# A planned instruction order for a convolution and two small networks on one core: durations of the plan, lent buffers, and the lag of the last network

## The chip, the core and the metric

The kernel runs on one core of one Trainium2 chip. The metric is the device time of one execution in microseconds (us). A core has five engines that run side by side and each take their instructions strictly in the order in which the program gives them: PE (TensorE, matrix products; its weight loads are listed apart as PEld), DVE (VectorE), ACT (ScalarE), POOL (GpSimd) and SP (SyncE, which here only issues transfers). Engines wait for each other through semaphores. PE writes into PSUM, eight banks of 128 x 512 32-bit values; all else lies in SBUF.

## The reference

For two sequences of 4160 tokens with 192 channels, three layers follow each other (shapes are batch, token, channel):

```python
# 1: a weighted sum over a window of 7 tokens, weights by softmax, 8 heads of 24 channels
w = exp(wg - max(wg)) ; w = w / (sum(w) + 1e-9)
x = einsum("bshk,bskhg->bshg", w, windows(x))
# 2: a mix of each token with the one before it, a network of width 1024, a gate
xk = mu_k * x + (1 - mu_k) * x_prev ; xr = mu_r * x + (1 - mu_r) * x_prev
x = sigmoid(xr @ w_r) * (maximum(xk @ w_k, 0) ** 2 @ w_v)
# 3: a network of width 1024 with a convolution of three tokens as its gate
h = maximum(x @ w_in, 0)
g = sigmoid(sum(conv_w[k] * shifted(h, k) for k in range(3)))
out = (h * g) @ w_out
```

Everything is 32-bit floating point.

## The kernel before

The tokens of each sequence are cut into ten tiles of 256, 220, seven times 476, and 352 tokens. A product is made precise by splitting its operands into a high and a low part (the cast to `fp32r` is the high part, the subtraction after it the low part), so that each product of the two networks takes five matmuls instead of two. For one tile and one batch the work is this:

- **attention**: POOL multiplies the window rows by the softmax weights and folds the seven products (`prod`, `prod`, `prod`, `tok`), four slots for a tile of 476 tokens.
- **mixing** (three for a tile: `u` is 0, 2 or 1; the second in time is `u = 2`): PE transposes the tokens into a bank `pa` ("flip"), ACT copies the shifted part (`att`), DVE subtracts, DVE writes two mixes (`mk`), ACT casts the high part (`xA`, or `rm` when `u = 2`), POOL subtracts for the low part. When `u = 2`, SP then moves both parts into `xB`.
- **gate_r** and **moe1**, eight steps: five matmuls into a bank `pa` (`xA`, `xB` with `wk`), two ACT passes, an ACT cast and a DVE subtraction (`s`), and five matmuls with `wv` into the banks `am`, `ar`. `gate_r` makes five matmuls with `wr` and a sigmoid (`r`) for each of two channel blocks. `mix_out` multiplies both and leaves `x`.
- **moe2**, eight steps: five matmuls into a bank `pc` (`x` with `wi`), relu and a scaled copy on ACT, two DVE taps of the convolution, a sigmoid, a product, a cast and a subtraction (`g`), and five matmuls with `wo` into `bm`, `br`. `store` copies both banks (`att`, `om`) and SP sends them out.

In the first 90 us or so the weights come in as well: sixteen chunks pass through `stage`, a buffer of 4096 32-bit columns, on ACT, DVE and PE.

No loop sets the order. Every piece of work is filed with a step number (`at(t, fn)`; a moe1 step is one unit of `t`, a tile 16 units). The class `Program` records all instructions, then `schedule` plays them through with a table of durations (`cost`, line 80): at each moment each engine takes, among its instructions that are ready by the table, the one with the lowest step number. The instructions are given to the chip in the order of the start times that come out. The table is thus no duration on the chip, but it decides in which order each engine's queue stands. Two numbers of the plan matter here: moe2 of a tile is filed `LAG` = 11 steps behind its moe1 (lines 31, 841, 844), and the tiles of each ring are handed out in turn, so a write into a tile has to wait for the last reader of what stood there. `mk` has two tiles, `att` two, `om` one (lines 256 to 264). When the weights are through, columns of `stage` from 864 on lie idle, but for two tiles lent to moe2 (`q_r`, line 287).

All instructions are recorded by one helper, so every row of the profile has the line L178; rows are told apart by the names of their tiles.

Of the kernel before, what the change touches and what calls it, by code (L numbers as in the profile page):

```python
# [9 lines left out]
F32R = mybir.dt.float32r  # L10
U32 = mybir.dt.uint32
# [8 lines left out]
NMAX = max(SIZES)  # L20
# [7 lines left out]
PAD = KS - 1  # L28
WIN = KS * DM
NF = DFF // 128  # L30
LAG = 11

S_LAG, G_LAG = 3.25, 4.75
DONE = 16 * NTILE + S_LAG - 0.95
ALONE = 7


def f(ap):
    return ap.bitcast(F32)


class Program:
# [26 lines left out]
    def region(self, ap):  # L69
# [7 lines left out]
            return ap.tensor.name, 0, 128, 0, 512  # L77
        return ap.tensor.name, p0, p0 + dims[0][1], f0, f0 + sum(s * (c - 1) for s, c in dims[1:]) + 1

    def cost(self, eng, method, out, ins, pointer):  # L80

        n = self.count(out)
        src = [self.space(x) for x in ins]
        if method == "dma_start":
            return 0.6, 0.0
        if eng == "PE":
            if method == "matmul" and ins[0].dtype == F32:
                n *= 4.6
            busy = max(n * 0.00045 + 0.002, 0.109)
            return busy, busy + 0.24  # L90
        if eng == "ACT":
            near = bool(src) and src[0] == "PSUM"
            p = 0.1 if pointer else 0.0
            return (0.06 if near else 0.09) + p + n / 1200, (0.2 if near else 0.24) + p + n / 1200
        if eng == "DVE":
            if method == "tensor_reduce":
                return 0.05 + self.count(ins[0]) / 515, 0.15 + self.count(ins[0]) / 515
            if method == "reciprocal":
                return 0.07 + n / 160, 0.2 + n / 160
            if method in ("tensor_scalar", "tensor_copy", "memset") and "PSUM" not in src:  # L100
                return 0.07 + n / 1920, 0.2 + n / 1920
            stt = method == "scalar_tensor_tensor"
            return (0.13 if stt else 0.07) + n / 960, (0.26 if stt else 0.2) + n / 960
        if eng == "POOL":
            busy = 0.15 + (n / 455 if method == "tensor_tensor" else n / 270)
            return busy, busy + 0.1
        return 0.6, 0.6

# [84 lines left out]
def conv_moe_kernel(ctx: ExitStack, tc: tile.TileContext, xp, wg_first, wg_rest, mus, w_k, w_v, w_r, w_in, conv_w, w_out, out):  # L193
# [11 lines left out]
    def ring(name, n, shape, dtype=F32):  # L205
        return Ring([new(f"{name}{j}", shape, dtype) for j in range(n)])

    def bank(name):
        t = ps.tile([128, 512], F32, name=name)
        prog.spaces[t.tensor.name] = "PSUM"  # L210
        return t

    W = NMAX + 4
# [42 lines left out]
    att_r = ring("att", 2, [128, NMAX])  # L256
    mk_r = ring("mk", 2, [128, NMAX])
# [6 lines left out]
    om_r = ring("om", 1, [128, W])  # L264
# [7 lines left out]
    for j in range(4):  # L272
        n = soft_at[j + 1] - soft_at[j]
# [7 lines left out]
    am_r, ar_r, bm_r, br_r = (Ring([bank(x)]) for x in ("am", "ar", "bm", "br"))  # L281
# [3 lines left out]

    spare = f(stage)[:, 2 * (soft_at[4] - soft_at[3]) * NH:]
    q_r = Ring([spare[:, j * W:(1 + j) * W] for j in (0, 1)])
    pt_r = Grow(pc_r.tiles, (16 * NTILE, pa_r.tiles))
    ht_r = Grow(h_r.tiles, (16 * NTILE, mk_r.tiles))
    gt_r = Grow(g_r.tiles, (DONE, s_r.tiles))  # L290
# [3 lines left out]
    def at(t, fn, hold=0.0):  # L294
        plan.append((t, len(plan), fn, hold))
# [205 lines left out]
    def mixing(i, u, t, dt_):  # L501
        N, P, e = SIZES[i], PART[i], EXTRA[i]
        c = 1 if u >= 2 else 0
        O = slice(64 if u == 4 else 0, 64 if u == 3 else 128)
        st = {}

        def flip():
            p = pa_r()
            st["p"] = p[O, e:e + N]
            st["q"] = p  # L510
            x = tok_t[i]
            k, n = ((0, 128), (256, 128), (128, 128), (128, 64), (128, 128))[u]

            for l in reversed(range(SLOTS[i])):
                PE.transpose(p[0:n, l:l + SLOTS[i] * (P - 1) + 1:SLOTS[i]], x[:, l, k:k + n], ident)

        def shifted(fn):
            a = att_r()[O, :N]
            if e:
                fn(a, st["q"][O, e - 1:e + N - 1])  # L520
            else:
                fn(a[:, 1:N], st["q"][O, 0:N - 1])
            return a

        def m0():
            a = st["d"] = shifted(ACT.copy)
            DVE.tensor_tensor(a, a, st["p"], op=ALU.subtract)

        def m1(k):
            st[k] = ar_r.tiles[0][:, 256 * k:256 * k + 256] if i == 0 else mk_r()  # L530
            col = 2 * k + c
            own = slice(col, col + 1)
            if i < 2:
                a = shifted(lambda y, x: ACT.activation(y, x, ACTF.Copy, scale=onemu[O, own]))
                DVE.scalar_tensor_tensor(out=st[k][O, :N], in0=st["p"], scalar=mu[O, own], in1=a, op0=ALU.mult, op1=ALU.add)
            else:
                DVE.scalar_tensor_tensor(out=st[k][O, :N], in0=st["d"], scalar=onemu[O, own],
                                         in1=st["p"], op0=ALU.mult, op1=ALU.add)

        def hi(k):  # L540
            if u < 2:
                x = xA_r[k]()
                xin[i, u, k, 0] = x
            else:
                x = rm_r[k]().unsqueeze(1)
            st["h", k] = x
            ACT.copy(x[O, 0, :N], st[k][O, :N])

        def lo(k):
            x = st["h", k]  # L550
            y = x[O, 1, :N] if u < 2 else (mk_r() if i == 0 else st[k])[O, :N].bitcast(F32R)
            (POOL if i else DVE).tensor_tensor(y, st[k][O, :N], f(x[O, 0, :N]), op=ALU.subtract)
            if u >= 2:
                for b in range(NB) if u == 2 else (u - 3,):
                    z = xB_r[k]()
                    xin[i, b, k, 1] = z
                    own = slice(64 * b, 64 * b + 64)
                    oth = slice(64 - 64 * b, 128 - 64 * b)
                    SP.dma_start(out=f(z[own, :N]), in_=f(x[own, 0, :N]))
                    SP.dma_start(out=f(z[oth, :N]), in_=f(y[own] if u == 2 else y))  # L560

        at(t, flip)
        if i >= 2:
            at(t + 0.1 * dt_, m0)
        at(t + 0.2 * dt_, lambda: m1(0))
        at(t + 0.3 * dt_, lambda: m1(1))
        at(t + 0.4 * dt_, lambda: hi(0))
        at(t + 0.5 * dt_, lambda: lo(0))
        at(t + 0.6 * dt_, lambda: hi(1))
        at(t + 0.7 * dt_, lambda: lo(1))  # L570


# [122 lines left out]
    def moe2(i, b, fi, t):  # L695
# [28 lines left out]
        def c6():  # L724
            st["q"] = q_r() if i >= ALONE else st["p"]
            DVE.tensor_tensor(st["q"][:, :N], st["h"][:, 1:N + 1], st["p"][:, :N], op=ALU.mult)
# [6 lines left out]
        def c8():  # L733
            g = st["g"]
            (POOL if i >= ALONE else DVE).tensor_tensor(g[:, 1, :N], st["q"][:, :N], f(g[:, 0, :N]), op=ALU.subtract)

# [17 lines left out]
    def store(i, b, t):  # L754
        N = UNIT[i]
        last = i == NTILE - 1
        a = 1 if i == 1 else 0
        n = N + (1 if last else 0)
        t0 = STARTS[i] - OFFSET[i] - 1
        st = {}  # L760

        def e0():
            st["b"] = att_r()[0:64]
            ACT.copy(st["b"][:, :n], acc2["r"][64:128, :n])

        def e1():
            st["m"] = om_r()
            ACT.copy(st["m"][:, :n], acc2["m"][:, :n])
            SP.dma_start(out=out[b, 0:128, t0 + a:t0 + n], in_=st["m"][:, a:n])

        def e2():
            DVE.tensor_tensor(st["b"][:, :n], acc2["r"][0:64, :n], st["b"][:, :n], op=ALU.add)
            SP.dma_start(out=out[b, 128:192, t0 + a:t0 + n], in_=st["b"][:, a:n])

        at(t, e0)
        at(t + 0.1, e1)
        at(t + 0.2, e2)
# [36 lines left out]
    for j in range(NTILE - 3):  # L814
        a, b = (sum(slots[3:3 + k]) for k in (j, j + 1))
# [3 lines left out]
    a = slots[3]  # L819
# [6 lines left out]
    for i in range(NTILE):  # L826
# [6 lines left out]
        for b in range(NB):  # L833
# [4 lines left out]
            for fi in range(NF):  # L838
                moe1(i, b, fi, t + fi)
                if i:  # L840
                    moe2(i, b, fi, t + fi + LAG)
            mix_out(i, b, t + S_LAG + 7.27)
            if i:
                store(i, b, t + LAG + G_LAG + 7.27)

# [70 lines left out]
```

## Time and profile before

| | |
|---|---|
| median of three timed runs | 749.13 us (748.6 to 750.31) |
| the profiled execution | 749.3 us, of which the span from first to last instruction is 747.5 us |
| busy share of the span | PE 95%, PEld 81%, ACT 87%, DVE 78%, POOL 73% |
| mean granted clock of TensorE | 0.992 of its full 2.4 GHz |
| matmuls in the trace | 3473 |

Busy shares are means over stages with different limits. PE's matmuls overlap in the trace, so a busy PE is not always a PE at its full pace; how many matmuls start in a stretch tells the pace. The trace has the table of busy times by stretch, who waited for whom, and the instructions in order of time.

### The profile page before, as it was taken

To read this page: it belongs to the slowest core of one execution; us is meant where nothing else is said; L and a number is where in the kernel's file an instruction comes from. 1 tells how busy PE (TensorE), PEld (TensorE's weight loads), DVE (VectorE), ACT (ScalarE), POOL (GpSimd) and SP (SyncE) were. 2 spreads that over 40 slices of the span, in tenths; PEclk is the share of its full clock that TensorE was granted. 3 is DMA by queue.
4 is the path that set the end of the run, shared out by engine and by line. 5 is a ranking of instruction groups with operands and counts; after the bars stand their busy time and mean duration, and the time that the engine had idled before them with its cause. 6 is when DMAs were issued, how large, how long until landed. Compare 5 with 4: busy or idle time off the path is not lost.

```text
span 747.5 us, 10554 instructions
## 1 busy us (share of the span) xinstructions
PE 711.2 (95%) x3473; PEld 606.9 (81%) x3473; DVE 581.2 (78%) x985; ACT 650.0 (87%) x1388; POOL 546.7 (73%) x398
## 2 busy tenths in 40 slices
PE   3898888999999999989999999999999999999996
PEld 2677777888788888878888888888888888889995
DVE  5656968879998978787878787879786767676775
ACT  2588779999989899988989998999899989989986
POOL 3799999997899999999999999996113333333334
PEclk9999999999999999999999999999999999999999
DMA  7678212011211140213120410130003000200000
GB/s 227 171 248 241 75 54 52 6 68 54 72 54 24 49 126 1 72 53 74 53 73 1 126 48 20 48 73 1 20 1 73 0 21 1 59 1 20 1 20 30
DMA packets 18791, 45.09 MB, mean 60 GB/s; under 512 B 2992, under 2 KB 14256, under 8 KB 18608
## 3 DMA queue, kind: packets, MB, share of 16 engines
q1 hardware_dynamic: 18736, 44.41, 20.3%
q8 instruction: 27, 0.44, 0.3%
q14 instruction: 28, 0.23, 0.1%
HBM read 27.40 MB, written 6.39 MB: 45 GB/s over the span
## 4 chain that ended last, share of the span: by engine, by line
PE 48%; POOL 35%; ACT 6%; DVE 4%; issue 4%; DMA 2%; SPq 0%; ACTq 0%; POOLq 0%; DVEq 0%
POOL prod L178 28%; PE pa L178 15%; PE pc L178 10%; PE bm L178 7%; PE am L178 6%; PE br L178 5%; PE ar L178 4%; POOL tok L178 3%; POOL xA L178 2%; DVE pc L178 1%; ACT pa L178 1%; POOL mk L178 1%; DMA stage<-in_moe_w_in_dram 1%; DMA stage<-in_moe_w_k_dram 1%; DVE mk L178 1%
## 5 line engine op out<-in xcount | busy, mean ns | idle before, releaser
L178 DVE SCALAR_TENSOR_TENSOR pc<-h,cw,pc 128x476 f32<-128x476 f32 (+1 forms) x276 | 194.6, 705 | 42.1 <-ACT pc L178 39.1
L178 POOL TENSOR_TENSOR prod<-rows,sw 128x1344 f32<-128x1344 f32 x70 | 216.4, 3093 | 12.6 <-DVE sw L178 10.5
L178 ACT ACTIVATE pa<-pa 128x476 f32<-128x476 f32 (+4 forms) x326 | 163.3, 504 | 29.6 <-PE pa L178 26.0
L178 POOL TENSOR_TENSOR prod<-prod 128x576 f32<-128x576 f32 (+1 forms) x132 | 161.8, 1225 | 9.0
L178 PE MATMUL am<-s,wv 128*128 128x476 f32 (+3 forms) x480 | 142.0, 356 | 2.9 <-ACT s L178 2.8
L178 PE MATMUL bm<-g,wo 128*128 128x476 f32 (+1 forms) x414 | 135.2, 379 | 2.1 <-ACT g L178 1.8
L178 PE MATMUL pa<-xA,wkA 128*128 128x476 f32 (+3 forms) x480 | 123.1, 361 | 3.7 <-DVE s L178 2.6
L178 POOL TENSOR_TENSOR g<-stage,g 128x476 fp32r<-128x476 f32 (+1 forms) x42 | 48.5, 1156 | 96.3 <-ACT g L178 76.0
L178 PE MATMUL pc<-x,wiA 128*128 128x478 f32 (+1 forms) x414 | 113.4, 379 | 0.9 <-ACT x L178 0.4
L178 DVE TENSOR_TENSOR s<-pa,s 128x476 fp32r<-128x476 f32 (+3 forms) x160 | 93.8, 586 | 21.6 <-ACT s L178 20.2
L178 PE MATMUL ar<-s,wv 128*128 128x476 f32 (+3 forms) x320 | 109.1, 355 | 0.0
L178 PE MATMUL br<-g,wo 128*128 128x476 f32 (+1 forms) x276 | 103.4, 376 | 0.0
L178 PEld LDWEIGHTS pa<-xA,wkA 128*128 128x128 f32 x480 | 83.8, 189 | 21.2 <-DVE s L178 7.1
L178 PEld LDWEIGHTS am<-s,wv 128*128 128x128 f32 x480 | 87.0, 188 | 15.0 <-ACT s L178 4.4
L178 ACT ACTIVATE pc<-h,cw 128x476 f32<-128x476 f32 (+1 forms) x138 | 92.0, 667 | 0.7
L178 ACT ACTIVATE h<-pc 128x478 f32<-128x478 f32 (+1 forms) x138 | 78.8, 571 | 12.5 <-PE pc L178 10.6
L178 PE MATMUL pa<-xB,wkB 128*128 128x476 f32 (+3 forms) x320 | 88.7, 357 | 0.0
L178 PEld LDWEIGHTS bm<-g,wo 128*128 128x128 f32 x414 | 76.8, 189 | 13.8 <-ACT g L178 2.7
L178 PEld LDWEIGHTS pc<-x,wiA 128*128 128x128 f32 x414 | 75.5, 189 | 15.3 <-DVE g L178 3.4
L178 ACT CAST s<-pa 128x476 fp32r<-128x476 f32 (+3 forms) x160 | 83.1, 520 | 1.5
L178 DVE TENSOR_TENSOR pc<-h,pc 128x476 f32<-128x476 f32 x96 | 62.8, 654 | 26.9 <-ACT pc L178 26.0
L178 PE MATMUL pc<-x,wiB 128*128 128x478 f32 (+1 forms) x276 | 81.7, 377 | 0.0
(135 smaller groups left out, 1170.0 us busy)
## 6 DMA issues: line engine op xcount, KB each, us to landing
rows<-in_x_dram SPq DMA_DIRECT2D x14, 960.0 KB, 4.6
xB<-rm SPq DMA_DIRECT2D x28, 119.0 KB, 2.3
xB<-mk SPq DMA_DIRECT2D x28, 119.0 KB, 2.3
out_dram<-om SPq DMA_DIRECT2D x14, 238.0 KB, 2.0
rows<-in_x_dram SPq DMA_DIRECT2D x4, 768.0 KB, 5.8
rows<-in_x_dram SPq DMA_DIRECT2D x2, 864.0 KB, 4.7
out_dram<-att SPq DMA_DIRECT2D x14, 119.0 KB, 2.2
stage<-in_moe_w_v_dram SPq DMA_DIRECT2D x4, 384.0 KB, 4.5
```

Of the source, the lines that this page charges most:

```text
L178: getattr(self.real[eng], method)(*a, **k)
```

## The change

It has three parts. The table of durations in `cost` gets other numbers: products of 32-bit operands on PE cost less (a factor of 3.75 for 4.6), single-source passes of DVE lose a double rate, POOL passes in place cost 0.08 us more, and ACT and DVE passes whose output lies on other partitions than their input get a surcharge. From step 20 on three rings are longer: `mk` gets two more tiles, `att` one, `om` one, all in the idle columns of `stage`. `LAG` goes from 11 to 12, so that moe2 and `store` of every tile are filed one step later.

```diff
-LAG = 11
+LAG = 12
+SPARE = 20
...
             if method == "matmul" and ins[0].dtype == F32:
-                n *= 4.6
+                n *= 3.75
...
-            if method in ("tensor_scalar", "tensor_copy", "memset") and "PSUM" not in src:
+            if method == "memset":
                 return 0.07 + n / 1920, 0.2 + n / 1920
...
+    mkt_r = Grow(mk_r.tiles, (SPARE, [spare[:, j * W:j * W + NMAX] for j in (2, 3)]))
+    attt_r = Grow(att_r.tiles, (SPARE, [spare[:, 4 * W:4 * W + NMAX]]))
+    omt_r = Grow(om_r.tiles, (SPARE, [spare[:, 5 * W:6 * W]]))
...
         def shifted(fn):
-            a = att_r()[O, :N]
+            a = attt_r()[O, :N]
...
-            st[k] = ar_r.tiles[0][:, 256 * k:256 * k + 256] if i == 0 else mk_r()
+            st[k] = ar_r.tiles[0][:, 256 * k:256 * k + 256] if i == 0 else mkt_r()
...
         def e0():
-            st["b"] = att_r()[0:64]
+            st["b"] = attt_r()[0:64]
...
-            st["m"] = om_r()
+            st["m"] = omt_r()
```

No instruction is added or taken away; PE has 3431 of them in both programs, DVE 987, ACT 1390, POOL 403, SP 173. What moves is their order, and the tiles that the mixes write.

First place: DVE in the second mixing of the sixth tile (`u = 2`, tile number 5). `mk`, `att`, `stage` are tiles of the rings, `s`, `g`, `pc` belong to moe1 and moe2. Before:

```order
L178 TENSOR_TENSOR att1_88<-att1_88,pa1_114 128x476
L178 TENSOR_TENSOR pc0_115<-h0_109,pc0_115 128x476
L178 SCALAR_TENSOR_TENSOR mk0_89<-att1_88,onemu_62,pa1_114 128x476
L178 TENSOR_TENSOR s0_105<-pa0_113,s0_105 128x476
L178 TENSOR_TENSOR g0_77<-pc0_115,g0_77 128x476
L178 SCALAR_TENSOR_TENSOR mk1_90<-att1_88,onemu_62,pa1_114 128x476
```

With the change, at the same place:

```order
L183 TENSOR_TENSOR stage_76<-stage_76,pa1_114 128x476
L183 SCALAR_TENSOR_TENSOR stage_76<-stage_76,onemu_62,pa1_114 128x476
L183 TENSOR_TENSOR pc1_116<-h1_110,pc1_116 128x476
L183 TENSOR_TENSOR s0_105<-pa0_113,s0_105 128x476
L183 SCALAR_TENSOR_TENSOR stage_76<-stage_76,onemu_62,pa1_114 128x476
L183 TENSOR_TENSOR g3_80<-pc1_116,g3_80 128x476
```

The mixes stand about where they stood, but they write into columns of `stage` instead of into `mk0` and `mk1`, which the first mixing of the same tile has just filled.

Second place: ACT at the end of the second tile and in the second mixing of the third (`u = 2`, tile number 2), around the one exponential of 448 columns that stands between sigmoids (`sw` is the softmax, `r00` the first gate of moe1, `rm` the high part that goes into `xB`). Before:

```order
L178 CAST s3_108<-pa1_114 128x220
L178 ACT_TABLE_LOAD
L178 ACTIVATE sw_112<-sw_112 128x448
L178 CAST rm00_91<-mk0_89 128x476
L178 ACT_TABLE_LOAD
L178 ACTIVATE r00_103<-pa0_113 128x220
```

With the change:

```order
L183 CAST g3_80<-pc1_116 128x476
L183 ACTIVATE pc0_115<-h0_109,cw_63 128x476
L183 CAST rm00_91<-mk0_89 128x476
L183 ACT_TABLE_LOAD
L183 ACTIVATE sw_112<-sw_112 128x448
L183 ACT_TABLE_LOAD
L183 ACTIVATE r00_103<-pa0_113 128x220
```

The cast of `rm` now stands ahead of the exponential and both table loads.

Third place: PE at that time, between the products of the two gates (`wr`), which use the same bank `pa0` one after the other. Before:

```order
L178 MATMUL pa0_113<-xB10_100,wrB_73 128x220 x2
L178 MATMUL pc0_115<-x2_0_74,wiA_68 128x478 x3
L178 MATMUL pc0_115<-x2_0_74,wiB_69 128x478 x2
L178 MATMUL pa1_114<-xA00_93,wkA_66 128x476 x3
L178 MATMUL bm_119<-g2_79,wo_71 128x476
L178 MATMUL br_120<-g2_79,wo_71 128x476
L178 MATMUL am_117<-s3_108,wv_70 128x220
L178 MATMUL ar_118<-s3_108,wv_70 128x220
L178 MATMUL pa0_113<-xA11_96,wrA_72 128x220 x3
```

With the change:

```order
L183 MATMUL pa0_113<-xB10_100,wrB_73 128x220 x2
L183 MATMUL pc1_116<-x2_0_74,wiA_68 128x478 x3
L183 MATMUL pc1_116<-x2_0_74,wiB_69 128x478 x2
L183 MATMUL bm_119<-g3_80,wo_71 128x476
L183 MATMUL br_120<-g3_80,wo_71 128x476
L183 MATMUL pa0_113<-xA11_96,wrA_72 128x220 x3
```

Seven matmuls lie between the two gates instead of twelve. Counted in PE's order from its start, the flip of that second mixing has 457 matmuls ahead of it before and 485 with the change, and the first matmul that reads its `xB` has 513 and 520. At the other end, PE has 18 passes with `wiB` left behind the last matmul of moe1 before, and 20 with the change (two for each step of moe2).

## Rows read from the trace of the kernel before

**Rows 1.** Busy time by stretch: us from the start, length, busy and count by engine, clock.
```profile
0.00:100.00 100.00, 77.57 (x436) 61.71 (x437) 67.48 (x145) 67.32 (x199) 81.77 (x63) 0.98 0.62 180
100.00:137.00 37.00, 33.40 (x178) 28.55 (x178) 29.79 (x53) 32.06 (x70) 34.80 (x27) 0.95 0.19 54
178.00:190.00 12.00, 11.09 (x50) 8.99 (x49) 10.26 (x18) 11.94 (x19) 5.25 (x6) 1.00 0.19 43
190.00:333.00 143.00, 142.92 (x666) 120.15 (x665) 124.53 (x202) 130.12 (x266) 138.42 (x93) 1.00 0.18 56
333.00:340.00 7.00, 4.91 (x16) 3.86 (x15) 4.40 (x7) 3.70 (x8) 7.00 (x7) 0.76 0.33 75
340.00:725.00 385.00, 384.41 (x1860) 335.94 (x1859) 296.33 (x482) 350.76 (x716) 230.58 (x172) 1.00 0.12 34
725.00:747.50 22.50, 15.98 (x87) 13.57 (x85) 14.16 (x28) 15.93 (x38) 9.22 (x10) 0.96 0.08 25
```

**Rows 2.** Waits of PE, 10 to 137 us: total, times, longest.
```profile
PE bm L178 <- DVE stage L178: 12.1, 3, 10.8
```

**Rows 3.** Instructions by time, 322 to 345 us: start, length, instruction, idle before it.
```profile
330.07 3.09 POOL L178 TENSOR_TENSOR prod<-rows,sw 128x1344 f32<-128x1344 f32 x1
...
333.12 2.34 POOL L178 TENSOR_TENSOR xA<-mk,xA 128x476 fp32r<-128x476 f32 x2
...
334.35 0.71 DVE L178 SCALAR_TENSOR_TENSOR mk<-att,onemu,pa 128x476 f32<-128x476 f32 x1 [2.33 <-POOL xA L178]
334.98 0.65 DVE L178 TENSOR_TENSOR s<-pa,s 128x476 fp32r<-128x476 f32 x1
...
335.68 1.27 PE L178 MATMUL pa<-xA,wkA 128*128 128x476 f32 x3 [2.09 <-DVE s L178]
```

**Rows 4.** Waits of DVE, 190 to 725 us.
```profile
DVE mk L178 <- POOL xA L178: 3.5, 3, 2.3
```

**Rows 5.** Instructions by time, 409 to 415 and 484 to 490 us.
```profile
412.05 0.71 DVE L178 SCALAR_TENSOR_TENSOR mk<-att,onemu,pa 128x476 f32<-128x476 f32 x1 [0.46 <-POOL xA L178]
...
413.38 0.91 PE L178 MATMUL pc<-x,wiA 128*128 128x478 f32 x3 [0.17 <-DVE g L178]
...
486.33 0.71 DVE L178 SCALAR_TENSOR_TENSOR mk<-att,onemu,pa 128x476 f32<-128x476 f32 x1 [0.68 <-POOL xA L178]
...
488.22 0.91 PE L178 MATMUL pa<-xA,wkA 128*128 128x476 f32 x3 [0.28 <-DVE s L178]
```

**Rows 6.** Instructions by time, 108 to 130 us.
```profile
113.35 0.60 PE L178 MATMUL pa<-ident,tok 128*128 128x128 f32 x4
...
116.19 1.33 DVE L178 SCALAR_TENSOR_TENSOR mk<-att,onemu,pa 128x476 f32<-128x476 f32 x2
...
116.94 1.28 ACT L178 ACT_TABLE_LOAD   x1
...
118.72 0.57 ACT L178 CAST rm<-mk 128x476 fp32r<-128x476 f32 x1
...
120.61 0.35 ACT L178 ACTIVATE r<-pa 128x220 f32<-128x220 f32 x1
...
121.01 0.59 PE L178 MATMUL pa<-xA,wrA 128*128 128x220 f32 x3 [0.22 <-ACT r L178]
...
124.76 0.59 PE L178 MATMUL pa<-xB,wkB 128*128 128x476 f32 x2
```

**Rows 7.** Busy time of all instructions between 98 and 137 us, by the same columns as Rows 1.
```profile
98.00:137.00 39.00, 35.00 (x189) 29.79 (x188) 31.50 (x57) 34.03 (x76) 36.72 (x29) 0.96 0.19 51
```

**Rows 8.** Instructions of PE by time, 714 to 719 us.
```profile
716.14 0.65 PE L178 MATMUL pa<-x,wiA 128*128 128x356 f32 x3
...
716.95 0.49 PE L178 MATMUL bm<-g,wo 128*128 128x354 f32 x2
...
717.77 0.48 PE L178 MATMUL am<-s,wv 128*128 128x352 f32 x2
```

**Rows 9.** Busy time by stretch near the end, same columns as Rows 1.
```profile
730.00:735.00 5.00, 4.58 (x26) 3.91 (x25) 3.96 (x9) 4.95 (x13) 2.84 (x3) 1.00 0.18 56
```

More of the change, by code (lines that the diff above doesn't have):

```diff
@@ L78, in region, with lane @@
         return ap.tensor.name, p0, p0 + dims[0][1], f0, f0 + sum(s * (c - 1) for s, c in dims[1:]) + 1
+    def lane(self, ap):
+        return ap.offset // ap.ap[0][0]
     def cost(self, eng, method, out, ins, pointer):
@@ L92, in cost @@
             near = bool(src) and src[0] == "PSUM"
-            p = 0.1 if pointer else 0.0
+            p = 0.12 if pointer or self.lane(out) != self.lane(ins[0]) else 0.0
             return (0.06 if near else 0.09) + p + n / 1200, (0.2 if near else 0.24) + p + n / 1200
@@ L99, in cost @@
                 return 0.07 + n / 160, 0.2 + n / 160
-            if method in ("tensor_scalar", "tensor_copy", "memset") and "PSUM" not in src:
+            if method == "memset":
                 return 0.07 + n / 1920, 0.2 + n / 1920
-            stt = method == "scalar_tensor_tensor"
-            return (0.13 if stt else 0.07) + n / 960, (0.26 if stt else 0.2) + n / 960
+            wide = 0.06 if method == "scalar_tensor_tensor" and ins[0].dtype != U32 else 0.0
+            far = 0.11 if self.lane(out) != self.lane(ins[0]) else 0.0
+            return 0.065 + wide + far + n / 960, 0.18 + wide + far + n / 960
         if eng == "POOL":
-            busy = 0.15 + (n / 455 if method == "tensor_tensor" else n / 270)
+            busy = (0.23 if ins and ins[0].tensor.name == out.tensor.name else 0.15) + (n / 455 if method == "tensor_tensor" else n / 900)
             return busy, busy + 0.1
@@ L550, in lo @@
             x = st["h", k]
-            y = x[O, 1, :N] if u < 2 else (mk_r() if i == 0 else st[k])[O, :N].bitcast(F32R)
+            y = x[O, 1, :N] if u < 2 else (mkt_r() if i == 0 else st[k])[O, :N].bitcast(F32R)
             (POOL if i else DVE).tensor_tensor(y, st[k][O, :N], f(x[O, 0, :N]), op=ALU.subtract)
```

## The prediction

> **What bounds the kernel now.** I read first the table of busy times by stretch, because the shares of the whole span (PE 95%) hide where PE stands still. The reader is to see three regions in it [rows 1]. In the first 137 us PE is busy for 77.57 + 33.40 = 110.97 us and so idle for 26.0; 10.8 of these lie ahead of its first product and are untouched here [rows 2], so 15.2 us of idle time are spread over the stretch in which weights still come in and the first, small tiles run. From 190 us on PE hardly stops: 666 matmuls start in 143 us, one every 143/666 = 0.2147 us, with 0.08 us idle, and from 340 to 725 us it is idle for 0.6. There, no other engine's waits cost anything, and a change can only win what interrupts this pace. The interruption is a single hole, 333 to 340 us, in which only 16 matmuls start and the clock falls to 0.76. At the end, from 725 us, PE is busy for 15.98 of 22.5 us.
>
> Next I read the instructions in order of time around the hole [rows 3]. POOL starts an attention product of 3.09 us at 330.07, and the low part `xA<-mk` of the first mixing stands behind it, from 333.12 on. The second mixing wants to write the same `mk` tile, the ring having two, so DVE waits 2.33 us for POOL with `s` of moe1 queued behind it, and PE, which needs the bank `pa` that this `s` reads, waits 2.09 us. Then the list of DVE's waits [rows 4]: three such waits in all, 3.5 us. The other two reach PE as 0.17 and 0.28 us [rows 5].
>
> **The change part by part.** *The longer rings.* With four tiles in `mk`, the second mixing writes tiles that the first has not touched; the space comes round again only two mixings later. The order shows this at the sixth tile: the mixes stand at about the same place of DVE's queue but write into `stage`. POOL's product still delays the low parts; the difference is that nothing of DVE is queued behind them any more. What is worth removing is the hole: 16 matmuls at the pace of 0.2147 are 3.44 us, so 7.00 - 3.44 = 3.56 us were lost there [rows 1], 2.09 as a wait and 1.47 at the lower clock behind it. With the two small waits the sum is 3.56 + 0.17 + 0.28 = 4.0 us. The bounds are 0 (another wait stands right behind) and 4.0; I take 4.0, because PE keeps its pace on both sides of the hole with the same neighbours, and after `mk` nothing in these rows is late: SP moves `xB` for moe1 of the next tile only, a flip's lead of more than three steps. The third tile for `att` and the second for `om` have no wait in these rows to remove: 0.
>
> The hole can be priced otherwise. The Trainium skill (Perfetto Trace Analysis, "Identifying the Most-Contended Engine") says that the busy share of matmuls is a poor measure of how near PE is to its limit, since they are pipelined, and that the share of weight loads is a better one. By it the loads were busy for 3.86 of 7 us, against 120.15/143 = 0.84 at full pace [rows 1], so the hole would be worth 7 - 3.86/0.84 = 2.4 us, the plain busy time 2.09, the count of matmuls 3.56. The sum would then end 1.2 us later; I stay with the count, since a matmul that starts is work done, whatever the clock.
>
> *The lag.* Every moe2 step is filed one step later, so one more step of moe2 is left when moe1 has ended (20 passes with `wiB` for 18). PE's work is the same in all; what counts is that this step moves from a stretch where PE is busy all the time into one where it is busy 15.98/22.5 = 0.71 of it [rows 1]. Ten matmuls of such a step take 717.77 - 716.14 = 1.63 us [rows 8]; at that share 1.63/0.71 = 2.30, so 0.67 us more. The bounds are 0 and 1.63. For nothing speaks that ACT, the engine that is full there (4.95 of 5 us with 13 instructions, 0.38 us each, so four for a step are 1.5 us [rows 9]), needs no longer than PE; for the whole step, that nothing else is left to overlap with it. I take 0.7.
>
> *The table.* It costs no time by itself. It draws the first 137 us anew, and there the 15.2 us of idle time are many waits of different chains, so the sign is open. One place can be read off the order. The second mixing of the third tile begins with a flip at 113.35 us, and the first matmul that reads its `xB` starts 11.4 us later, at 124.76 [rows 6]. With the change 28 more matmuls stand ahead of the flip and only 7 more ahead of that matmul. At 39.0/189 = 0.206 us for one [rows 7] that is 21 x 0.206 = 4.3 us less of other work between flip and use. Against it, the cast `rm` now stands ahead of the exponential and its table loads: before, it started at 118.72, while the first of the two mixes (1.33 us for both from 116.19) was done by about 116.9, so some 1.6 us come back. The lowest price of this place is 0 (PE had more waits than these in the chain and reaches it late anyway), the highest 4.3. For the whole start I take +0.5 us, little, because the plan behind the new order works with durations nearer to the rows; the ends are -4 (a quarter of the 15.2 us gone) and +5.8 (below).
>
> *The sum.* 749.3 (the profiled execution, 747.5 of it span) - 4.0 + 0.7 + 0.5 = **746.5 us**. The median of the runs shown is 749.13, 0.2 less, which I don't correct for.
>
> **The rivals.**
>
> *A. The start wins much.* The new table prices what was priced wrongly, and the weight chunks, gates and flips of the first 137 us interlock better. For it speaks that each wait there is a matter of order alone, against it that the chains (a chunk through ACT, DVE and PE, a gate behind a sigmoid) are no shorter. At a quarter of the idle time the start gives 3.8 instead of costing 0.5: 742.2; at half, 738.4.
>
> *B. Slower: the late flip.* The second mixing of the third tile is on the path: its chain takes the 11.4 us of the rows, the cast's new place doesn't help because POOL and SP behind it are as late as before, and PE stands for 4.3 us, above all at the second gate, whose bank waits for a sigmoid behind both table loads with seven matmuls of cover instead of twelve. A wait of 2.09 us was followed by 1.47 us lost at the lower clock [rows 1, 3]; here the same comes on top: 5.8 us. The result is 749.3 - 4.0 + 0.7 + 5.8 = 751.8. It decides from a loss of 4.6 us in the start on. Against it: PE's waits ahead of the flip can be shorter than they were, and the flip then comes earlier than its place in the row says.
>
> *C. No difference: the hole moves.* The rings are longer, but what DVE waited for is only the first of several. ACT is busy for 130.12 of 143 us at full pace [rows 1]; if it, or the one tile of `rm`, holds the same `s` back, the hole shrinks by half or not at all: 748.5 to 750.5. Against it: before and after the hole PE starts at full pace with the same load on ACT.
>
> **How the numbers follow.** What a measurement of this kernel can tell from no change is about 0.2%, 1.5 us, so faster is below 747.6 and slower above 750.6. The forecast, 744.5 to 748.2 with 746.5 in it, has 0.44: the price of the hole is well read, the start is not. A has 0.20, B 0.16, C 0.20. Faster takes A and most of the forecast, 0.60; slower takes B and a little of C, 0.17; the rest, 0.23, is no difference. The range goes from 741.5, which cuts off the better half of A, to 750.8, which cuts off most of B.
>
> **What would show it.** Right: in the list of DVE's waits behind 190 us no `mk` behind POOL's `xA`; between 190 and 725 us no stretch of a few us with a clock below 1.00, and less than 0.5 us idle on PE. The last stretch from the end of moe1 is longer by some 0.7 us, and ACT is still full in it. The idle time of PE between its first product and the end of the second tile is 15 us within four. Wrong: PE waiting on `r` or on `xB` for 2 us or more around 115 to 130 us (B); a hole at another tile with a low clock (C); an idle time in the start that differs by more than 4 us (A or B). What would upset all of it is a wait of PE at full pace that no row of before shows, since every such wait costs its length and the clock behind it.

## The result, and the profile after

| | before | with the change |
|---|---|---|
| median of four runs | 749.49 us (748.6 to 750.31) | 743.04 us (742.73 to 743.48) |
| ratio | | 0.9915, 95% interval 0.9897 to 0.9932 |
| profiled execution | 749.3 us, span 747.5 us | 743.48 us, span 741.7 us |

The change is faster by 6.4 us. Its 743.04 us lie 3.5 below the 746.5 that was predicted: inside the range, but below the 744.5 at which the likeliest case ended, and next to the 742.2 of rival A. The table of busy times by stretch, with the change (columns as in [rows 1]):

```profile
0.00:100.00 100.00, 77.25 (x437) 61.86 (x437) 67.95 (x146) 66.98 (x200) 78.56 (x60) 0.97 0.60 180
100.00:137.00 37.00, 33.57 (x178) 28.42 (x177) 29.23 (x51) 32.53 (x70) 34.73 (x26) 0.95 0.20 54
178.00:190.00 12.00, 12.00 (x58) 10.24 (x57) 9.31 (x15) 11.63 (x16) 8.08 (x8) 1.00 0.24 86
190.00:333.00 143.00, 142.65 (x666) 120.61 (x665) 125.22 (x209) 133.89 (x271) 137.22 (x93) 1.00 0.19 56
333.00:340.00 7.00, 7.00 (x34) 5.94 (x33) 5.24 (x9) 5.62 (x12) 6.78 (x5) 1.00 0.63 193
340.00:725.00 385.00, 384.91 (x1868) 336.70 (x1867) 299.52 (x488) 352.96 (x722) 235.42 (x175) 1.00 0.11 33
725.00:741.70 16.70, 10.49 (x52) 7.90 (x50) 8.71 (x18) 9.98 (x24) 6.58 (x7) 0.93 0.11 33
```

Counting the matmuls that have started shows where the time came from. Against [rows 1] there are 437 for 436 in the first 100 us, as many as before from 100 to 137, **58 for 50** from 178 to 190, 666 for 666 up to 333, and **34 for 16** in the place of the hole, at clock 1.00 for 0.76. (137 to 178 us has 191 in both.) At 340 us the changed kernel is thus 1 + 8 + 18 = 27 matmuls ahead, and 27 x 0.2147 = 5.8 us is the whole difference of the spans, 747.5 - 741.7. (Of the 8, six make up the pace of 0.2147, and two are the mix of shapes.) Behind 340 us nothing is gained in sum: the 8 further matmuls up to 725 stand there because the last tile, whose matmuls are shorter, begins earlier. So two thirds of the gain are the hole, and most of the rest is a stretch for which the prediction had no term. The start, from which rival A had its gain, gave one matmul, and so A is not what happened.

The waits of PE that are left between 137 and 718 us (total, times, longest):

```profile
PE pa L183 <- ACT r L183: 0.3, 1, 0.3
```

DVE has no wait for POOL's `xA` any more, where [rows 4] had three. The place of rival B, PE's waits from 119 to 126 us:

```profile
118.89 0.70 PE L183 MATMUL bm<-g,wo 128*128 128x476 f32 x2 [0.45 <-ACT g L183]
123.52 0.59 PE L183 MATMUL pa<-xA,wrA 128*128 128x220 f32 x3 [1.24 <-ACT r L183]
124.78 1.34 PE L183 MATMUL pa<-xA,wkA 128*128 128x476 f32 x3 [0.44 <-ACT r L183]
```

The second gate's wait for the sigmoid has grown from 0.22 us [rows 6] to 1.24, and the last row's 1.34 us for three matmuls, 0.91 for the same three behind the small wait of [rows 5], is the lower clock behind it. It is B's mechanism, at a quarter of its price, and the start as a whole lost nothing by it.

### The profile page after: what moved, and what is told of

It reads as the page before. It is cut to its first block, busy times and chain, and to the rows that moved or that the text cites. A ratio compares the mean times of both kernels' runs of the same rounds, so it can differ in the third digit from the quotient of the medians.

```text
span 741.7 us, 10552 instructions
## 1 busy us (share of the span) xinstructions
PE 708.9 (96%) x3473; PEld 606.4 (82%) x3473; DVE 579.6 (78%) x985; ACT 653.6 (88%) x1388; POOL 547.0 (74%) x398
## 4 chain that ended last, share of the span: by engine, by line
PE 80%; POOL 8%; ACT 5%; issue 3%; DVE 2%; DMA 1%; SPq 0%; POOLq 0%; ACTq 0%; DVEq 0%
PE pa L183 25%; PE pc L183 18%; PE bm L183 12%; PE am L183 11%; PE br L183 7%; PE ar L183 7%; POOL prod L183 5%; ACT pa L183 1%; DMA stage<-in_moe_w_k_dram 1%; POOL s L183 1%; ACT L183 1%; DVE stage L183 0%; POOL g L183 0%; POOL xA L183 0%; POOL tok L183 0%
## 5 line engine op out<-in xcount | busy, mean ns | idle before, releaser
L183 PE MATMUL bm<-g,wo 128*128 128x476 f32 (+1 forms) x411 | 133.6, 379 | 1.1 <-ACT g L183 0.8
```

The lines of the kernel that those rows point to most:

```text
L183: getattr(self.real[eng], method)(*a, **k)
```

## The experiments

Three of them put one part of the change into the kernel before, three leave one part out, two keep an order and take only the wait away, one leaves the other two rings out, two make the lag longer, and one is the kernel before once more. Ratios are to the kernel before, run beside each of them, with medians of 748.99 to 749.68.

| kernel | median, us | ratio, 95% interval |
|---|---|---|
| longer rings alone | 744.67 | 0.9941, 0.9926 to 0.9956 |
| new durations alone | 745.88 | 0.9951, 0.9933 to 0.9968 |
| lag of 12 alone | 754.33 | 1.0065, 1.005 to 1.008 |
| two more `mk` tiles, order of before | 743.3 | 0.992, 0.9907 to 0.9934 |
| rings and lag | 746.56 | 0.9962, 0.9949 to 0.9975 |
| rings and durations | 746.04 | 0.9957, 0.9941 to 0.9974 |
| durations and lag | 744.02 | 0.9931, 0.9913 to 0.9949 |
| the change, `mk` alone lent | 742.72 | 0.9911, 0.9895 to 0.9927 |
| the change, lag 13 | 745.3 | 0.9942, 0.9921 to 0.9963 |
| the change, lag 15 | 752.9 | 1.0049, 1.0027 to 1.0071 |
| two more `mk` tiles, order of the lag alone | 747.51 | 0.9976, 0.9966 to 0.9987 |

**The wait alone.** The two `mk` tiles are lent, but the plan counts each of them as one of the old tiles, too, so that it still believes in the wait. Every engine's order stays that of before, and only the tiles differ:

```diff
+    def regions(self, ap, step):
+        own = self.region(ap)
+        out = [own]
+        for name, lo, tile in self.lent:
+            if step >= SPARE and own[0] == name and lo <= own[3] and own[4] <= lo + NMAX:
+                out.append((tile, *own[1:3], own[3] - lo, own[4] - lo))
+        return out
...
-                name, p0, p1, f0, f1 = self.region(x)
+              for name, p0, p1, f0, f1 in self.regions(x, self.ops[i][4]):
...
+    prog.lent = [(stage.tensor.name, base + (2 + j) * W, mk_r.tiles[j].tensor.name) for j in (0, 1)]
...
-            st[k] = ar_r.tiles[0][:, 256 * k:256 * k + 256] if i == 0 else mk_r()
+            st[k] = ar_r.tiles[0][:, 256 * k:256 * k + 256] if i == 0 else mkt_r()
```

> The kernel before with the two lent tiles for mk alone, while the plan goes on as if the mixes had only the two old tiles (a lent tile counts as its old one in the plan's dependencies). Every engine's order is then that of before, and only the tile and with it the wait is another. Theory: the three waits of DVE's mk behind POOL's xA go, and with them the hole: 749.4 - 4.0 = 745.4 us, within 0.5, matmuls at full pace and clock 1.00 from 333 to 340 us. Rival (another wait stands right behind: ACT, the one tile of rm, or POOL's late low part for xB or xA): the hole shrinks to half or less of its loss removed, 747.4 to 749.4, and PE waits there on something else.

It ran in 743.3 us. Instructions in order of time at the sixth tile, in this kernel:

```profile
329.32 3.10 POOL L187 TENSOR_TENSOR prod<-rows,sw 128x1344 f32<-128x1344 f32 x1
...
331.19 0.70 DVE L187 SCALAR_TENSOR_TENSOR stage<-att,onemu,pa 128x476 f32<-128x476 f32 x1
331.81 0.64 DVE L187 TENSOR_TENSOR s<-pa,s 128x476 fp32r<-128x476 f32 x1
...
332.38 2.40 POOL L187 TENSOR_TENSOR xA<-mk,xA 128x476 fp32r<-128x476 f32 x2
332.69 0.80 PE L187 MATMUL pa<-xA,wkA 128*128 128x476 f32 x3
```

POOL's product stands where it stood in [rows 3] and is as long, and the low part comes right behind it as before. But DVE writes the second mixing 1.2 us before POOL has begun the first one's low part, `s` follows at once, and PE goes on. The table of busy times for the same kernel:

```profile
190.00:333.00 143.00, 142.93 (x666) 120.32 (x666) 125.44 (x205) 130.06 (x266) 138.60 (x93) 1.00 0.18 56
333.00:340.00 7.00, 7.00 (x34) 5.88 (x33) 4.92 (x9) 6.35 (x13) 6.92 (x7) 1.00 0.41 94
```

The stretch of the hole has 34 matmuls for 16: 18 x 0.2147 = 3.9 us, the 3.56 and a little more. With the order held, no other wait took the place, and rival C is out.

The gain of 6 us is larger than the 4.0 expected. As both kernels run the same instructions in the same order, matmul by matmul can be compared. In the kernel before, the last matmul ahead of the hole, and the first product behind it at the full pace:

```profile
333.21 0.38 PE L178 MATMUL br<-g,wo 128*128 128x476 f32 x1
...
339.50 0.81 PE L178 MATMUL pc<-x,wiA 128*128 128x478 f32 x3
```

The same two in the kernel with the lent tiles, and the one that [rows 5] has at 488.22 us:

```profile
332.46 0.38 PE L187 MATMUL br<-g,wo 128*128 128x476 f32 x1
...
334.94 0.81 PE L187 MATMUL pc<-x,wiA 128*128 128x478 f32 x3
...
482.77 0.82 PE L187 MATMUL pa<-xA,wkA 128*128 128x476 f32 x3
```

The lead is 0.75 us ahead of the hole, 4.56 behind it and 5.45 behind both small waits. So the hole was worth 3.81, and the two small waits 0.89 where their idle times sum to 0.45. One reason can be read off the rows: a row's idle time begins where the matmul before it is drawn to end, 0.38 us after its start, while at full pace the next one starts 0.2147 after it; each wait thus costs 0.17 us more than its idle time, 0.34 and 0.45 here. The rest of the lead is the 0.75 from the start and 0.6 behind 488 us.

**The kernel before, once more.**

> The kernel before once more, for a second trace of the same order. In the first the matmuls at 106 to 110.5 us ran at half the clock behind waits of 1.28 and 0.28 us; with the same order and the same waits the lent mk tiles alone had no half clock there, which is 1.6 us of their 6. If the fall of the clock at that place is a matter of each execution, this trace has the waits there and may have no half clock; the hole at 333 to 340 us and its 0.76 are there again. Rival (the place always has the half clock, and the lent tiles took it away): half clock at 106 to 110.5 again.

It took 748.54 us, with the same waits. Busy time by stretch, first in the first trace of before, then in the second:

```profile
30.00:45.00 15.00, 11.80 (x58) 8.97 (x58) 11.46 (x25) 12.01 (x38) 14.12 (x10) 0.89 0.50 139
106.00:111.00 5.00, 4.71 (x18) 4.11 (x19) 3.71 (x7) 2.49 (x6) 4.76 (x4) 0.66 0.36 121
```

```profile
30.00:45.00 15.00, 12.38 (x54) 9.61 (x55) 10.81 (x23) 10.97 (x33) 14.53 (x10) 0.77 0.57 155
106.00:111.00 5.00, 4.47 (x27) 3.94 (x28) 3.94 (x8) 3.92 (x10) 4.84 (x3) 1.00 0.32 103
333.00:340.00 7.00, 5.20 (x17) 4.43 (x18) 4.60 (x8) 4.49 (x9) 6.92 (x8) 0.76 0.44 100
```

With one order and the same waits (1.28 and 1.29 us at 106 us), the clock fell behind them in one execution (0.66) and not in the other (1.00). The hole and its 0.76 came both times. But from 30 to 45 us it is the second execution that had the lower clock for longer (0.77 for 0.89), and the kernel with the lent tiles had 0.77 there, too, and 0.83 from 55 to 65 us. So the clock at 106 us, to which the expectation put down 1.6 of the 6 us, is no account of the surplus. Against this second execution the lent tiles are 748.54 - 743.3 = 5.2 us faster; matmul by matmul they are 0.14 behind ahead of the hole, and the hole is again worth 3.8 and the two small waits 1.0.

**One part each.** The edits are those of the change's diff, each by itself.

> The kernel before with the three longer rings alone; durations of the plan and the lag as before. Theory (the hole at 333 to 340 us is a wait for the tile mk, nothing else): it goes with both small mk waits, 749.4 - 4.0 = 745.4 us, within 0.8; the start and the wait on the gate at 188 us stay as before. Rival (the hole is a matter of order and only the new durations or the lag remove it): 748 or more, with a hole of 2 us or more of PE somewhere behind 190 us.

> The kernel before with the new durations of the plan alone. Theory: mk still has two tiles, so DVE still waits for POOL's xA and a hole of about 2 us with a low clock behind it stays behind 190 us; the start is drawn anew at a net of 0 and the gate's wait at 188 us goes (1.3): 747.5 to 749.5. Rival (the new durations give the better order and are the gain): 743 to 745.5 with no hole. Second rival (the lag, not the durations, took the wait at 188 away): that wait is still there and the time is 749 or more.

> The kernel before with the lag of 12 alone. Theory: the hole stays, the last stretch costs between 0 and 0.7 more, so 749 to 750.3. Rival (moe2 and its store, one step later, no longer meet the attention product and the second mixing on POOL, DVE and ACT): the hole goes or halves, 745 to 747.5. Second rival (the wait on the gate at 188 us goes by the lag): that row is gone and the time is about 1.3 below what the rest gives.

The rings alone do what was expected (744.67, no hole, 34 matmuls from 333 to 340 us, the wait on the gate still there in part). The other two surprised. The durations alone are nearly as good, 745.88: the hole at 333 us is gone with two tiles, and one wait of 1.7 us on `s` has come up at 225 us, behind a pass of 3.07 us on DVE (`stage<-stage`, at 220.60) and not behind a tile. DVE has no wait for POOL's `xA` behind 137 us: the first mixing's writes (328.58 and 330.32 us) come when POOL's product is nearly done, the low part follows at 330.61, and the second mixing writes from 333.49 on. The lag alone is slower by 4.8. DVE's waits on `mk` in it:

```profile
258.46 0.71 DVE L178 SCALAR_TENSOR_TENSOR mk<-att,onemu,pa 128x476 f32<-128x476 f32 x1 [0.88 <-POOL xA L178]
...
334.59 0.71 DVE L178 SCALAR_TENSOR_TENSOR mk<-att,onemu,pa 128x476 f32<-128x476 f32 x1 [1.99 <-POOL xA L178]
...
412.16 0.71 DVE L178 SCALAR_TENSOR_TENSOR mk<-att,onemu,pa 128x476 f32<-128x476 f32 x1 [2.67 <-POOL xA L178]
```

The wait of the sixth tile is still there, and the seventh tile's has grown from 0.46 us [rows 5] to 2.67. To see whether these are again the tile and nothing else, the order of the lag alone was kept and only the tiles were lent, by the same edit as above:

> The lag of 12 alone, which gave 754.3, with the two lent tiles for mk and a plan that goes on as if there were two (a lent tile counts as its old one in the plan's dependencies), so that every engine's order is that of the lag alone. That order has three waits of DVE's mk behind POOL's xA, of 0.88, 1.99 and 2.67 us, at which PE loses 0.6, 1.7 and 4.2 us. Theory (these are the tile and nothing else): 6.5 less, 747.8 within 1, and the losses at 206 to 210 us and in the start, which the lag brought too, stay. Rival (another wait stands behind the tile, as POOL is as late as before): less than half of it goes, 751 or more.

It ran in 747.51, 6.8 less than the lag alone for 6.5 expected; compared matmul by matmul, the two traces differ by 0.7, 1.9 and 4.1 us at the three waits, 6.6 in sum. So in two orders taking the wait away, without moving an instruction, gave at least what its rows said.

**One part left out.**

> The change without its new durations: longer rings and the lag of 12. The lag alone gave 754.3, with three waits of mk and PE losses at 210, 336 and 414 us. Theory (each of these is the ring of mk, and the order only decides where it bites): with four mk tiles all three go, 8 to 9 us less: 744.5 to 746.5. Rival (the lag brings ACT, POOL and the second mixing together whatever the ring): one of the three stays at over 1 us and the time is 748 or more.

> The change without its lag: longer rings and new durations, lag 11. Theory (no hole is left in any order once mk has four tiles; lag and durations are then worth less than 1.5 us each): 742.5 to 745. Rival (the lag is part of the gain, by the wait on the gate at 188 to 193 us): 0.8 to 1.5 slower than the whole change, 744 to 745, with a gate wait of about 1 us behind 178 us. The prediction's own term: 0.7 faster than the whole change.

> The change without its longer rings: new durations and the lag of 12. Theory: mk has two tiles again and DVE waits for POOL's xA at one to three places behind 190 us; each costs PE 1.5 to 4: 746.5 to 750. Rival (the new durations know what POOL takes and the order avoids the wait): 743 to 745, and then the rings are not what the change lives on.

The last is the one that counts. With new durations, the lag of 12 and only two `mk` tiles the time is 744.02, and its interval overlaps that of the whole change. POOL's instructions at the sixth tile in it:

```profile
321.97 2.53 POOL L182 TENSOR_TENSOR prod<-prod 128x576 f32<-128x576 f32 x2
324.46 2.39 POOL L182 TENSOR_TENSOR xA<-mk,xA 128x476 fp32r<-128x476 f32 x2
326.82 0.59 POOL L182 TENSOR_TENSOR tok<-prod 128x192 f32<-128x192 f32 x1
327.37 3.09 POOL L182 TENSOR_TENSOR prod<-rows,sw 128x1344 f32<-128x1344 f32 x1
330.43 2.38 POOL L182 TENSOR_TENSOR mk<-mk,rm 128x476 fp32r<-128x476 f32 x2
```

In this order the low parts of the first mixing stand ahead of the product of 3.09 us, not behind it, and the old tiles are free in time. The theory for this run is wrong, its rival right. In the change the low parts stand ahead of the product, too:

```profile
325.39 2.39 POOL L183 TENSOR_TENSOR xA<-mk,xA 128x476 fp32r<-128x476 f32 x2
...
328.29 3.09 POOL L183 TENSOR_TENSOR prod<-rows,sw 128x1344 f32<-128x1344 f32 x1
```

So there the hole is removed twice over, by the order and by the tiles, and either is enough.

The eight corners, medians in us (before is the one of the first comparison):

| | two `mk` tiles | longer rings |
|---|---|---|
| old durations, lag 11 | 749.49 | 744.67 |
| old durations, lag 12 | 754.33 | 746.56 |
| new durations, lag 11 | 745.88 | 746.04 |
| new durations, lag 12 | 744.02 | 743.04 |

The parts do not add. The rings are worth 4.8, 7.8, nothing and 1.0 (the last not clear of the spread); the lag costs 4.8 or 1.9 with the old durations and gives 1.9 or 3.0 with the new ones. With two tiles the four orders lie 10.3 us apart, with the longer rings 3.5.

**What the lag does at 178 to 190 us.** PE in order of time at the end of this stretch, in the kernel before:

```profile
187.08 0.37 PE L178 MATMUL ar<-s,wv 128*128 128x476 f32 x1
188.33 0.91 PE L178 MATMUL pa<-xA,wrA 128*128 128x476 f32 x3 [0.88 <-ACT r L178]
```

ACT there, in the same kernel:

```profile
182.62 2.36 ACT L178 ACTIVATE sw<-sw 128x2576 f32<-128x2576 f32 x1
...
185.96 1.28 ACT L178 ACT_TABLE_LOAD   x1
187.25 0.55 ACT L178 ACTIVATE pc<-pc 128x476 f32<-128x476 f32 x1
187.71 0.56 ACT L178 ACTIVATE r<-pa 128x476 f32<-128x476 f32 x1
```

And PE with the lag alone, at the same place:

```profile
187.98 0.37 PE L178 MATMUL ar<-s,wv 128*128 128x476 f32 x1
188.20 0.37 PE L178 MATMUL bm<-g,wo 128*128 128x476 f32 x1
188.44 0.91 PE L178 MATMUL pa<-xA,wrA 128*128 128x476 f32 x3
```

ACT is taken by the one large exponential with a table load on either side, and the second gate's bank waits for a sigmoid behind them. With the lag of 12 the sigmoid comes no earlier (187.83 for 187.71 us), but 17 matmuls stand between the two gates for 14, two of the three further ones with `wo`, and PE is busy until it comes. None of the six kernels with lag 12 has a wait of PE on `r` above 0.4 us behind 137 us; those with lag 11 have 0.9 (before, and the lent tiles alone), 0.2 (rings alone), and 1.0 with the new durations, which have theirs at 193 us, behind this stretch, with or without the longer rings.

**The other rings.** The change with `att` and `om` as before, `mk` alone lent:

> The whole change, but only mk gets the lent tiles; att keeps two and om one. Theory (no wait in the trace of before was one for att or om): within 0.7 of the whole change, 742.4 to 743.9. Rival (with the other order att's two tiles, shared by three mixings and two stores, hold back a mixing or a store): 745 or more, and ACT waits for DVE or SP ahead of an att or om copy, with PE waiting behind it.

742.72, no different from the change. The third `att` tile and the second `om` tile do nothing here, as predicted.

**A longer lag.** The change with `LAG = 13` and `LAG = 15`:

```diff
-LAG = 12
+LAG = 13
```

> The whole change with a lag of 13 instead of 12: one more step of the last network is left behind the end of moe1. By the prediction's term for the lag each such step costs 0.7 us (0 to 1.63): the stretch from the last product with wv to the last matmul has ten matmuls more and PE loses 0.5 to 0.7 more in it. Rival (that stretch was already limited by PE and ACT alike, and a step more only makes it longer by its own work, which is missing elsewhere): no more loss. No mk wait and no wait on a gate of over 0.5 us behind 178 us in either case. Time by the first 743.7, by the second 743.0, and any order drawn anew may bring 1 to 3 us in the start.

> The whole change with a lag of 15, three steps more. By the prediction's term the end costs 2.1 us more than in the change (745.1); by the rival, that a step there takes its own work and nothing more, 743.0 with the usual 1 to 3 us of a new order in the start. Read in the stretch behind the last product with wv: how many matmuls it has and how long it is.

Busy time from the last product with `wv` to the last matmul, for the kernel before, the change, lag 13 and lag 15:

```profile
720.86:743.07 22.21, 20.11 (x112) 17.68 (x111) 17.68 (x36) 18.39 (x46) 10.36 (x11) 1.00 0.05 14
```

```profile
713.33:737.23 23.90, 22.16 (x122) 19.26 (x121) 19.21 (x39) 20.51 (x50) 11.29 (x12) 1.00 0.04 13
```

```profile
713.51:739.45 25.94, 24.31 (x132) 22.31 (x131) 20.48 (x42) 21.78 (x53) 12.16 (x13) 0.93 0.07 22
```

```profile
715.65:746.04 30.39, 27.88 (x153) 25.82 (x151) 23.95 (x48) 25.75 (x63) 14.02 (x15) 0.94 0.07 22
```

Each step adds ten matmuls. The change's step made the stretch 1.69 us longer, its own work of 1.63 [rows 8] and no more; the step to 13 took 2.04, and the two to 15 took 2.2 each, all at a lower clock behind a wait of 1.3 us for ACT's `s` (at 733.76 and 740.41 us). With lag 13 the time is 2.3 us above the change, with lag 15 9.9, far more than either theory had, and most of it is lost elsewhere. PE's waits with lag 13 at 124 to 131 us:

```profile
125.86 0.91 PE L183 MATMUL pa<-xA,wkA 128*128 128x476 f32 x3 [1.86 <-ACT r L183]
129.77 0.70 PE L183 MATMUL am<-s,wv 128*128 128x476 f32 x2 [2.15 <-ACT s L183]
```

From 100 to 137 us lag 13 starts 168 matmuls and lag 15 starts 165, for 178 with the change; from 190 to 333 lag 15 starts 645 for 666. Lag 13 waits for a sigmoid and a cast there, and lag 15 too (1.16 and 2.36 us). The reading is that a late moe2 is missed there as work that covers what ACT owes; that it is the order drawn anew, and not the lag as such, no run excludes.

## Why the prediction was right, and where not

*The hole (-4.0).* Right in mechanism and size. 18 matmuls are 3.9 us; with the order held fixed the hole alone gave 3.8, and nothing stood behind the wait. The two small waits were put too low, 0.45 for the 0.89 that they gave there. The count of matmuls is the measure: by the share of weight loads the hole would have been worth 2.4. The loads took longer at the lower clock as well (3.86 us for 15 in the hole, 0.26 each, against 120.15 for 665, 0.18), so this share, too, counts slowness as work. The share of weight loads is one of two measures that the Trainium skill (Perfetto Trace Analysis, "Identifying the Most-Contended Engine") prefers to the busy share; the other is the matmul work done in a stretch, and the count of matmuls comes near to that one. What the prediction did not say is that the new order removes the same hole without any tile: its sentence that POOL's product still delays the low parts is true of the order of before, and false of the change, where `xA<-mk` runs ahead of it.

*The lag (+0.7).* Mis-sized. The tail got longer by the step's own work, 1.69 us with the 1.63 of [rows 8], so the lower bound of 0 that the prediction named was the value (0.06). But the tail was not what the lag is about. The step asked what one more step costs where PE is not full, and not what it covers where PE waits: at 188 us it covers a gate.

*The start (+0.5, sign open).* It came out as nothing: one matmul more by 137 us, 0.2 us. The second gate's wait did grow, by 1.0 us, with the clock behind it, and the rest of the start made up for it. The change's execution had the lower clock for longer from 30 to 45 us (0.77 for 0.89), so its start may be worth a little more than this 0.2 us. With other orders the same place cost more. PE at the second gate with rings and durations (lag 11), and with rings and lag (old durations):

```profile
123.68 0.59 PE L183 MATMUL pa<-xA,wrA 128*128 128x220 f32 x3 [2.74 <-ACT r L183]
```

```profile
119.57 0.84 PE L179 MATMUL pa<-xA,wrA 128*128 128x220 f32 x3 [3.42 <-ACT r L179]
```

So rival B was a real case; the whole change escaped it.

*What was missing.* The 12 us from 178 to 190. The row stood in [rows 1], with 50 matmuls where the pace of 0.2147 would have made 56 and with 0.9 us idle, and the prediction passed from the first 137 us to "from 190 us on" without a term for it. There the change gained 8 matmuls, 8 x 0.2147 = 1.7 us (1.3 without the two that are the mix of shapes). Against the profiled execution, 743.48, the sum was 3.0 us too high: this 1.7, the 0.7 for the lag, and 0.7 for the start (0.5 put down as a loss, 0.2 gained), less the 0.1 by which the hole and the small waits, 3.9 by the count, were put too high. That the result lies in the range is in part luck: the room below 744.5 had been made for a gain in the start, which did not come.

*Open.* Which number of the new durations moves `xA<-mk` ahead of the product was not tried. And since the order comes from a play of all durations at once, no run here says whether the gain of the new durations with lag 12 comes from better numbers or from this one order; lag 11 and lag 13 with the same durations and rings are 2 to 3 us slower. No run beat the change by more than its uncertainty.

## What to carry to other kernels

Where a planned order meets a short ring, price the ring by itself: keep the order, lend the tile, and the wait's own worth shows; a new order can move or remove the same wait, and the two gains do not add. In the four orders tried, a longer ring made the kernel less sensitive to the order (3.5 us between them for 10.3), which is worth having even where today's order does not need it. When a wait is priced from a trace, count from the pace at which matmuls start, since the idle time in a row leaves out the overlap. Before shifting a stage, look at every stretch in which PE waits, and ask what the shifted work covered there, not only what it costs at the end.

## What was not expected of the hardware

The same order with the same wait of 1.3 us at 106 us had the half clock behind it in one execution and full clock in another (0.66 and 1.00 over the same 5 us, 18 and 27 matmuls, so 9 x 5.00/27 = 1.7 us); a wait of 2.09 us at 335 us had the lower clock both times. From 30 to 45 us it was the other way round (0.89 and 0.77), and the spans lie only 0.7 us apart. At one place a profile can therefore carry a term of over a microsecond that belongs to no instruction, and a comparison of two profiles has to look whether the waits or only the clock behind them differ. The Trainium skill (TensorE: Matmul & The Clock Gate, "What's actually happening") says that the interval over which the array's activity is watched runs freely and does not start with the kernel, and that this is why the place at which the clock rises varies between runs. The two traces show that the fall varies as well.
